# Where k and v of a batch are projected in a fused attention and feed-forward kernel

## The chip, the core and the metric

The kernel runs on one core of a Trainium2 chip. The core's engines work through their own instruction queues: PE (TensorE) multiplies matrices into PSUM, ACT (ScalarE) and DVE (VectorE) read PSUM and write SBUF, POOL (GpSimd) and SP issue transfers. PSUM has eight banks of 128 partitions by 512 fp32 values. The time of a run is the device time of one execution in microseconds, and the kernel's time is the median over runs.

## The reference

For 8 batches, 8 heads, 1024 positions and head dimension 64, with a sequence projection to 64 rows:

```python
k_proj = np.einsum('ks,bhsd->bhkd', E, k)
v_proj = np.einsum('ks,bhsd->bhkd', F, v)
scores = q @ k_proj^T / sqrt(64)
attn   = softmax(scores)
x      = attn @ v_proj            # heads side by side: 8192 x 512
h1, h2 = x @ w1, x @ w2           # 512 x 1024 each
out    = np.maximum(h1, h2) @ w_out   # 8192 x 512, float32
```

## The kernel before

**What is computed.** max(h1, h2) is h2 + relu(x (w1 - w2)), so the kernel forms wd = w1 - w2 and m = w2 w_out once; each block of positions then needs an *up* product, g = relu(x wd), and a *down* product, out = [g, x] [w_out; m]. Both are done as seven block products instead of eight (p1, p2, p6, p5, p7, p3, p4, in this order), from sums of blocks of x (`sums_x`) and of g (`sums_g`) that DVE forms beforehand, S(0) to S(3) of each. Operands are f16.

**Units and half units.** The 16 *units* are (batch, half of the positions), numbered n = 0 to 15. While unit n goes through its down products, unit n + 1 goes through its up products, and the attention of later positions is done in between. A unit in the middle is cut into two halves h = 0 and 1. The order of the work is written out by hand as a list of *slots*:
- `P`: a down product is cut in three *pieces* of four matmuls; 21 pieces make the unit, P0 to P20 below. The last piece of a product also issues what takes the result away. P0 to P2 are p1, P3 to P5 are p2, P6 to P8 are p6.
- `U`: the seven up products of a half, U0 to U6, four matmuls each.
- `G`: one attention *group* (`step_group`): 16 score matmuls for the next group, 8 for the softmax's denominators, 16 for the values of the present one. All use tiles of 64 rows by 32 columns of PE.

A half is: some pieces, G, some pieces, then U0, piece, U1, piece, ... U6. The pair in `for h, (x, y)` gives the pieces before and after G. Up to now it is (2, 2) in the first half and (2, 3) in the second, so a first half runs P0 P1 G P2 P3 U0 P4 U1 P5 U2 P6 U3 and so on.

Extra work is hung on slots with `at_slot(key, step)`; it is issued behind the slot's own work, in the order of the calls in the source. Every engine runs its instructions in the order of issue.

**PSUM.** Banks 0 and 1 belong to the down products, banks 2 and 3 to the up products, which share them with the group's scores. In odd units p1 of down is in bank 1 and p2 in bank 0; bank 0 was last read by ACT at the end of the unit before (L827). In the first half p1 and then p6, p7, p4 of up go to bank 2; p2 and then p5 and p3 to bank 3. U0's result is copied by ACT (`keep`, L610) before U2 adds onto the same bank; U1's result is added to it by DVE (L651) before U3 starts afresh in bank 3. The scores' two exps (L368) free banks 2 and 3 for U0 and U1. The other four banks are a ring of two double tiles, `att_banks`, for denominators (read by ACT's Ln, L389, issued within the group) and values (read by DVE at U2, L397).

ACT's queue in a first half is thus: two exps, Ln, the copy of P2's result, the copy of U0's result, the inversion of the denominators (L393), and further copies.

**k and v of a batch.** `step_kv` multiplies k and v by the projections in 16 matmuls of 512 columns, k into partitions 0 to 63 and v into 64 to 127 of one bank, in tiles of 128 rows by 64 columns. For batches b = 3 to 7 it is hung on U1 in the first half of unit n = 2b - 3 (n = 3, 5, 7, 9, 11) and uses a tile of the attention ring. ACT casts k out of the bank and writes it twice (L198), and SP issues a DMA transpose from there to `kpt` (L230), which the scores of G in the second half need. DVE casts v out of the bank (L206) and copies it to partitions 0 to 63 (L207); these two are put off by one slot (`return finish_v`). POOL waits for the transposes of q and for the second copy of k (`step_gate`) before it issues the loads of the next batch.

**DVE's sums.** S(0) of g and S(2) of x are hung on the last up slot of the unit before, S(1) of g on P0.

Of the kernel before, what the change touches and what calls it, by code (L numbers as in the profile page):

```python
# [16 lines left out]
def kernel(  # L17
# [12 lines left out]
    nc = tc.nc  # L30

    B, H, S, D = q.shape
    KP = E.shape[0]
# [25 lines left out]
    def mm_bank(dtype=FP32, n=None):  # L59
        if n is None:  # L60
            n = turn.pop(0)
            turn.append(n)
        return ps.tile([128, 512 if dtype == FP32 else 1024], dtype, tag=f"mm{n}", name="mm_ps")

    def att_banks(dtype=FP32):
        return ps.tile(
            [128, 2, 512 if dtype == FP32 else 1024], dtype, tag="att", bufs=2, name="att_ps"
        )
# [49 lines left out]
    for g in range(2):  # L118
        for w_sb, w in ((w2_sb, moe_w2), (w1_sb, moe_w1)):
            nc.gpsimd.dma_start(  # L120
                out=w_sb.rearrange("p (g z) f -> p g z f", z=2)[:, g, :, 0:256],
                in_=w.rearrange("(g p z) f -> p g z f", p=128, z=2)[:, g, :, 0:256],
            )
    for w_sb, w, f0, f1 in (
# [3 lines left out]
        for z in range(2):  # L128
            nc.gpsimd.dma_start(
                out=w_sb.rearrange("p (g z) f -> p g z f", z=2)[:, :, z, f0:f1],  # L130
                in_=w.rearrange("(g p z) f -> p g z f", p=128, z=2)[:, :, z, f0:f1],
# [22 lines left out]
    for i in range(2):  # L154
        eft_ps = mm_bank()
        for c in range(NC):
            nc.tensor.transpose(
                out=eft_ps[:, c * KP : (c + 1) * KP],
                in_=ef_sb[:, i].rearrange("k (p c) -> k c p", c=NC)[:, c, :],
# [3 lines left out]
        eng = nc.scalar.copy if i else nc.vector.tensor_copy  # L163
# [9 lines left out]


    def step_kv(t, h0=0, h1=H, which="kv", att=False, dma=False, copy=nc.vector.tensor_copy):
        kv_ps = att_banks()[:, 0, :] if att else mm_bank()
        n = (h1 - h0) * D
        both = which == "v"
        nh = 2 if both else h1 - h0
        for h in range(0, h1 - h0, nh):  # L180
            for c in range(NC):
                for w in which:
                    i = "kv".index(w)
                    for r in range(2) if both else (i,):
                        nc.tensor.matmul(  # L185
                            out=kv_ps[r * KP : (r + 1) * KP, h * D : (h + nh) * D],
                            lhsT=eft[i][:, c, :],
                            rhs=t[w][:, h0 + h : h0 + h + nh, c, :],
                            start=(c == 0), stop=(c == NC - 1),
                        )  # L190
        fl = lambda ap: ap[:, h0:h1].rearrange("p h z d -> p (h z d)")
        zd = lambda ap: ap.rearrange("p (h d z) -> p h z d", d=D // 2, z=2)
        if "k" in which:
            eng = nc.vector.tensor_copy if which == "k" else nc.scalar.copy
            kp = t["kp"][:, h0:h1]
            k_ps = kv_ps[0:KP, 0:n].rearrange("p (h d) -> p h d", d=D)
            if dma:
                eng(out=kp, in_=k_ps[:, :, None, :].broadcast_to([KP, h1 - h0, 2, D]))  # L198
                step_kpt_dma(t)
            else:  # L200
                eng(out=kp[:, :, 0, :], in_=k_ps)
        if both:
            copy(out=t["vp"][:, h0:h1], in_=zd(kv_ps[:, 0:n]))
        elif "v" in which:
            def finish_v():
                nc.vector.tensor_copy(out=t["vp"][KP:128, h0:h1], in_=zd(kv_ps[KP:128, 0:n]))  # L206
                nc.vector.tensor_copy(out=fl(t["vp"][0:KP]), in_=fl(t["vp"][KP:128]))  # L207

            if att:
                return finish_v  # L210
            finish_v()
# [17 lines left out]
    def step_kpt_dma(t):  # L229
        nc.sync.dma_start_transpose(  # L230
            out=t["kpt"], in_=t["kp"].rearrange("p h r d -> p (h r d)")
        )
# [235 lines left out]
    U = {(b, o): {"n": n, "b": b, "o": o, "t": tiles[b]} for n, (b, o) in enumerate(units)}  # L468
# [371 lines left out]
    t = tiles[0]  # L840
    new_attn(t)
    new_xt(t)
    step_kv(t, 0, 4, "k")
    warm(2)
    step_kpt(t, 0, 4)
# [5 lines left out]
    step_sc(t, 0, 1)  # L851
    warm(2)
    step_kv(t, 4, 8, "k")
    step_dn(t, 0, 0)
    warm(2)
# [7 lines left out]
    step_sc(t, 1, 0)  # L863
    step_sc(t, 1, 1)
    step_kv(t, 0, 4, "v")
    step_dn(t, 1, 0)
    step_inv(t, 1, 0)
# [48 lines left out]

    for n, key in enumerate(units):
        downs = down_steps(U[key], n == last)  # L920
        if n in (0, last):
            for p, pieces in enumerate(downs):
                slots += [(("P", n, p, i), x) for i, x in enumerate(pieces)]
            continue
        pieces = [(("P", n, p, i), x) for p, x in enumerate(downs) for i, x in enumerate(x)]
        ups = [*up_steps(U[units[n + 1]])]
        for h, (x, y) in enumerate(((6, 1), (2, 1)) if n == 1 else ((2, 2), (2, 3))):
            slots += pieces[:x]
            slots.append((("G", n, h), lambda: None))
            slots += pieces[x : x + y]  # L930
            del pieces[: x + y]
            for i in range(7):
                slots.append((("U", n, h, i), ups.pop(0)))
                if i < 6 - ((n, h) == (1, 0)):
                    slots.append(pieces.pop(0))
        assert not pieces and not ups
# [3 lines left out]
    def at_slot(key, s, *a):  # L940
        steps.setdefault(key, []).append(lambda: s(*a))
# [11 lines left out]
    t = tiles[1]  # L953
    at_slot((0, 22), new_attn, t)
    at_slot((0, 22), lambda: turn.__setitem__(slice(None), [2, 3]))
    for n, x in enumerate((
# [3 lines left out]
        key = ("P", n // 15, (n - 1) // 2 % 7, (n - 1) % 2) if n else (0, 22)  # L960
# [22 lines left out]
    t = tiles[2]  # L983
# [8 lines left out]
    for b in range(3, B):  # L992
        t = tiles[b]
        n = 2 * b - 3
        key = ("U", n - 1, 1, 5)
        at_slot(key, new_attn, t)
        at_slot(key, step_qt_dma, t, 0, H // 2)
        at_slot(key, step_qt_dma, t, H // 2, H)
        at_slot(("U", n, 0, 1), step_kv, t, 0, H, "kv", True, True)
        at_slot(("U", n, 0, 6), step_gate, t, "qt", H - 1)  # L1000
        at_slot(("U", n, 0, 6), step_gate, t, "kp", H - 1, 1)
        at_slot(("U", n, 0, 6), loads, b + 1, "k", "v", "q")
# [4 lines left out]
    for i, (new, old) in enumerate(zip([*groups[1:], none], groups)):  # L1007
        n, h = divmod(i + 2, 2)
# [8 lines left out]
    for n, (b, o) in enumerate(units):  # L1017
        u = U[b, o]

        if b == 0:  # L1020
            where = ()
        elif n == 2:
            where = (("P", 1, 1, 1), 0), (("P", 1, 1, 2), 1), (("P", 1, 2, 0), 2), (("U", 1, 0, 1), 3)
        else:
            where = tuple((("U", n - 2, 1, k), i) for k, i in ((6, 2), (3, 0), (4, 1), (5, 3)))
        for key, i in where:
            at_slot(key, sums_x, u, (i,))

        if n:
            end = ("U", n - 1, 1, 6) if n > 1 else ("P", 0, 6, 1)  # L1030
            m = 0 if n == last else 2
            for key, i in (end, 0), (("P", n, 0, 0), 1), (("P", n, 1, m), 2), (("P", n, 2, m), 3):
                at_slot(key, sums_g, u, (i,))

    pending = []
# [40 lines left out]
```

## Time and profile before

| | us |
|---|---|
| median of 6 runs (322.13 to 323.4) | 322.49 |
| the profiled execution | 322.27 |
| its span, first to last instruction | 320.5 |
| PE busy | 313.8 |
| DVE busy | 236.2 |
| ACT busy | 210.1 |
| POOL busy | 40.9 |
| start of the projection of batches 3 to 7 | 101.88, 137.50, 173.13, 208.75, 244.38 |

The starts of the projection are those in the chain that ended last. A timeline line holds start, duration, engine, source line, operation, output and inputs, the shapes, and how many instructions are merged in the line; in brackets stands how long the engine was idle before and which engine released it. The granted clock of PE was 0.999 of full speed.

### The profile page before, as it was taken

What the parts mean: (1) busy time and instruction counts of PE and PEld (TensorE: products, weight loads), DVE (VectorE), ACT (ScalarE), POOL (GpSimd) and SP (SyncE); (2) the same over time, 40 slices, a digit from 0 to 9 for tenths busy, and PEclk for the clock granted to TensorE, in tenths of its full rate; (3) what the DMA queues carried; (4) which work ended last, traced back from release to release, by engine and by line L of the source; (5) the groups of instructions that cost most, each with busy time, mean ns of one, the idle gap of its engine ahead of it and who ended that gap; (6) DMA issues with size and microseconds to landing.
All of it is one profiled execution on the core that took longest, in us unless ns stands there. A gap on an engine that the chain in (4) does not pass through costs nothing.

```text
span 320.5 us, 9138 instructions
## 1 busy us (share of the span) xinstructions
PE 313.8 (98%) x3910; PEld 250.9 (78%) x3910; DVE 236.2 (74%) x420; ACT 210.1 (66%) x374; POOL 40.9 (13%) x63
## 2 busy tenths in 40 slices
PE   8979999999999999999999999999999999999996
PEld 3554587878887888878887888878887888888885
DVE  1356789887967796876967796976967696969683
ACT  1376742767776777667776777667777777765541
POOL 8259102003000400021000400030000000000000
PEclk9999999999999999999999999999999999999999
DMA  7999999999959999799999899899969231303033
GB/s 142 206 200 189 200 205 203 207 192 155 206 107 162 176 208 245 198 194 160 232 209 215 159 204 245 207 164 177 230 133 215 51 100 36 100 33 101 33 101 130
DMA packets 76408, 53.14 MB, mean 166 GB/s; under 512 B 29520, under 2 KB 76240, under 8 KB 76368
## 3 DMA queue, kind: packets, MB, share of 16 engines
q0 software_dynamic: 30944, 28.31, 56.3%
q1 hardware_dynamic: 45056, 23.80, 31.0%
q8 instruction: 30, 0.49, 0.6%
q10 hardware_dynamic: 368, 0.46, 0.6%
q14 instruction: 10, 0.08, 0.1%
HBM read 57.15 MB, written 16.78 MB: 231 GB/s over the span
## 4 chain that ended last, share of the span: by engine, by line
PE 91%; DMA 6%; DVE 0%; POOL 0%; issue 0%; POOLq 0%; DVEq 0%
PE mm_ps L728 47%; PE mm_ps L636 27%; PE mm_ps L422 4%; PE att_ps L185 4%; DMA big<-in_moe_w_dram 4%; PE att_ps L285 3%; DMA q_sb<-in_q_dram 3%; PE mm_ps L273 2%; PE mm_ps L524 2%; PE mm_ps L244 1%; PE att_ps L447 0%; DVE o_sb L821 0%; PE mm_ps L447 0%; POOL k_sb L98 0%; PE att_ps L273 0%
## 5 line engine op out<-in xcount | busy, mean ns | idle before, releaser
L610 ACT COPY p_sb<-mm_ps 128x512 f32<-128x512 f32 x179 | 101.4, 593 | 44.4 <-PE mm_ps L636 27.7
L728 PEld LDWEIGHTS <-big 128*128 128x128 f16 x768 | 73.5, 98 | 12.2 <-issue 3.6
L728 PE MATMUL mm_ps<-T_sb,big 128*128 128x256 f16 x576 | 77.7, 273 | 0.0
L651 DVE TENSOR_TENSOR gt_sb<-mm_ps,p_sb 128x512 f16<-128x512 f32 x56 | 38.5, 688 | 43.4 <-PE mm_ps L636 43.3
L636 PE MATMUL mm_ps<-big,big 128*128 128x256 f16 x336 | 50.4, 272 | 0.0
L636 PEld LDWEIGHTS <-big 128*128 128x128 f16 x448 | 43.8, 98 | 5.1
L728 PE MATMUL mm_ps<-wo_sb,gt_sb 128*128 128x256 f16 x256 | 42.8, 273 | 0.0
L728 PEld LDWEIGHTS <-gt_sb 128*128 128x128 f16 x376 | 35.2, 98 | 9.0 <-issue 5.0
L636 PEld LDWEIGHTS <-wd_sb 128*128 128x128 f16 x336 | 32.9, 98 | 3.8
L636 PE MATMUL mm_ps<-xt_sb,wd_sb 128*128 128x256 f16 x224 | 33.6, 273 | 0.0
L368 ACT ACTIVATE ex_sb<-mm_ps 128x512 f16<-128x512 f32 x50 | 27.2, 596 | 8.8 <-PE att_ps L285 7.5
L397 DVE TENSOR_TENSOR xt_sb<-att_ps,ld_sb 128x1024 f16<-128x1024 f32 x26 | 31.7, 1219 | 0.1
L758 DVE TENSOR_TENSOR o_sb<-mm_ps,p_sb 128x512 f32<-128x512 f32 x32 | 21.9, 685 | 9.3 <-PE mm_ps L728 7.3
L236 POOL COPY junk<-qt_sb 1x1 f16<-1x1 f16 x6 | 2.4, 402 | 172.9 <-DMA qt_sb<-q_sb 172.9
L728 PE MATMUL mm_ps<-m_sb,xt_sb 128*128 128x256 f16 x128 | 24.4, 273 | 0.0
L697 ACT ACTIVATE gt_sb<-mm_ps 128x512 f16<-128x512 f32 x28 | 16.8, 600 | 9.0 <-PE mm_ps L636 9.0
L654 DVE TENSOR_SCALAR gt_sb<-gt_sb 128x512 f16<-128x512 f16 (+1 forms) x60 | 21.1, 352 | 2.1
L596 DVE TENSOR_TENSOR big<-gt_sb 128x1024 f16<-128x1024 f16 x32 | 21.9, 684 | 0.1
L728 PE MATMUL mm_ps<-wo_sb,big 128*128 128x256 f16 x128 | 21.5, 272 | 0.0
L728 PE MATMUL mm_ps<-T_sb,gt_sb 128*128 128x256 f16 x120 | 20.3, 273 | 0.0
L728 PEld LDWEIGHTS <-xt_sb 128*128 128x128 f16 x188 | 18.4, 98 | 2.2
L651 DVE TENSOR_TENSOR gt_sb<-p_sb 128x512 f16<-128x512 f32 x28 | 19.1, 682 | 0.7 <-ACT p_sb L610 0.6
(104 smaller groups left out, 432.4 us busy)
## 6 DMA issues: line engine op xcount, KB each, us to landing
out_dram<-o_sb SPq DMA_DIRECT2D x62, 256.0 KB, 2.7
k_sb<-in_k_dram POOLq DMA_DIRECT2D x7, 1024.0 KB, 9.7
v_sb<-in_v_dram POOLq DMA_DIRECT2D x7, 1024.0 KB, 16.1
q_sb<-in_q_dram POOLq DMA_DIRECT2D x5, 1024.0 KB, 23.1
q_sb<-in_q_dram POOLq DMA_DIRECT2D x6, 512.0 KB, 15.5
big<-in_moe_w_dram POOLq DMA_DIRECT2D x12, 128.0 KB, 6.3
k_sb<-in_k_dram POOLq DMA_DIRECT2D x2, 512.0 KB, 8.3
v_sb<-in_v_dram POOLq DMA_DIRECT2D x4, 256.0 KB, 14.1
```

Source lines behind the costliest of these rows:

```text
L185: nc.tensor.matmul(out=kv_ps[r * KP : (r + 1) * KP, h * D : (h + nh) * D], lhsT=eft[i][:, c, :], rhs=t[w][:, h0 + h : h0 + h + nh, c, :], ...
L368: nc.scalar.activation(out=t["ex", g, j][:, e, :], in_=banks[e], func=ACTF.Exp, scale=scale)
L397: nc.vector.tensor_tensor(out=x_out(t, g, j).rearrange("q z o n -> q o z n"), in0=at_ps.rearrange("q o (z n) -> q o z n", z=2), in1=ld[:, ...
L422: nc.tensor.matmul(out=h_ps, lhsT=wd_sb[:, r, fb * 128 : (fb + 1) * 128], rhs=t["xt"][:, r, :, j * W : (j + 1) * W], start=(r == 0), stop= ...
L596: nc.vector.tensor_tensor(out=S(i), in0=S(0) if x is None else x, in1=y(), op=op)
L610: copy(out=x, in_=bank)
L636: nc.tensor.matmul(out=bank[:, m * W : (m + 1) * W], lhsT=w_[:, n_, (2 * d + m) * 128 : (2 * d + m + 1) * 128], rhs=a[:, n_, :], start=(n ...
L651: nc.vector.tensor_tensor(out=c_blk(j, c), in0=two(x), in1=two(y), op=ALU.add)
L654: nc.vector.tensor_scalar_max(ap, ap, 0.0)
L697: nc.scalar.activation(out=out, in_=in_, func=ACTF.Relu)
L728: nc.tensor.matmul(out=bank[i][:, 0:CH] if two_banks else bank[:, i * CH : (i + 1) * CH], lhsT=a(c)[:, i * 128 : (i + 1) * 128], rhs=w_(c) ...
L758: nc.vector.tensor_tensor(out=o_sb, in0=two(x), in1=two(y), op=ALU.add)
```

## The change

For batches 3 to 7 the projection moves from U1 to G in the first half of the same unit, ahead of the group's own matmuls. It uses bank 0 instead of a tile of the attention ring. k is cast by DVE instead of ACT, once instead of twice, and DVE makes the second copy in SBUF; the DMA transpose is issued behind that. The copies are no longer put off by a slot. The order on DVE is: k cast, v cast to partitions 64 to 127, second copy of k, v copy to partitions 0 to 63. In these five units S(1) of g moves from P0, and S(2) of x from the last up slot of the unit before, to the slot of G, behind the copies. The pieces around the two groups become (2, 1) and (3, 3), so that the first half runs P0 P1 projection G P2 U0 P3 U1 P4 U2 P5 U3 P6 and so on.

```diff
     def step_kv(t, h0=0, h1=H, which="kv", att=False, dma=False, copy=nc.vector.tensor_copy):
-        kv_ps = att_banks()[:, 0, :] if att else mm_bank()
+        kv_ps = att_banks()[:, 0, :] if att else mm_bank(n=0 if dma else None)
...
         if "k" in which:
-            eng = nc.vector.tensor_copy if which == "k" else nc.scalar.copy
+            eng = nc.vector.tensor_copy if which == "k" or dma else nc.scalar.copy
             kp = t["kp"][:, h0:h1]
-            k_ps = kv_ps[0:KP, 0:n].rearrange("p (h d) -> p h d", d=D)
-            if dma:
-                eng(out=kp, in_=k_ps[:, :, None, :].broadcast_to([KP, h1 - h0, 2, D]))
-                step_kpt_dma(t)
-            else:
-                eng(out=kp[:, :, 0, :], in_=k_ps)
+            eng(out=kp[:, :, 0, :], in_=kv_ps[0:KP, 0:n].rearrange("p (h d) -> p h d", d=D))
...
                 nc.vector.tensor_copy(out=t["vp"][KP:128, h0:h1], in_=zd(kv_ps[KP:128, 0:n]))
+                if dma:
+                    nc.vector.tensor_copy(out=kp[:, :, 1, :], in_=kp[:, :, 0, :])
+                    step_kpt_dma(t)
                 nc.vector.tensor_copy(out=fl(t["vp"][0:KP]), in_=fl(t["vp"][KP:128]))
...
+    kv_units = range(3, 2 * B - 4, 2)
...
-        for h, (x, y) in enumerate(((6, 1), (2, 1)) if n == 1 else ((2, 2), (2, 3))):
+        cut = ((6, 1), (2, 1)) if n == 1 else ((2, 1), (3, 3)) if n in kv_units else ((2, 2), (2, 3))
+        for h, (x, y) in enumerate(cut):
...
-        at_slot(("U", n, 0, 1), step_kv, t, 0, H, "kv", True, True)
+        at_slot(("G", n, 0), step_kv, t, 0, H, "kv", False, True)
...
-            where = tuple((("U", n - 2, 1, k), i) for k, i in ((6, 2), (3, 0), (4, 1), (5, 3)))
+            two = ("G", n - 1, 0) if n - 1 in kv_units else ("U", n - 2, 1, 6)
+            where = ((two, 2), *((("U", n - 2, 1, k), i) for k, i in ((3, 0), (4, 1), (5, 3))))
...
-            for key, i in (end, 0), (("P", n, 0, 0), 1), (("P", n, 1, m), 2), (("P", n, 2, m), 3):
+            one = ("G", n, 0) if n in kv_units else ("P", n, 0, 0)
+            for key, i in (end, 0), (one, 1), (("P", n, 1, m), 2), (("P", n, 2, m), 3):
                 at_slot(key, sums_g, u, (i,))
```

## The prediction

> **What bounds the kernel now.** I read the page's shares and its chain first, then the timeline of each engine through one of the five half units that the change touches (batch 4, unit 5; the other four repeat it at a period of 35.6 us).
>
> ```profile
> PE 313.8 (98%) x3910; PEld 250.9 (78%) x3910; DVE 236.2 (74%) x420; ACT 210.1 (66%) x374; POOL 40.9 (13%) x63
> ...
> PE 91%; DMA 6%; DVE 0%; POOL 0%; issue 0%; POOLq 0%; DVEq 0%
> ```
>
> PE carries the chain after the start-up, and in the steady part nothing keeps it waiting. So each 0.1 us that PE loses or saves in a touched half unit is 0.5 us of the kernel; time on ACT, DVE or POOL counts only where PE has to wait for it.
>
> PE around the group and the projection:
>
> ```profile
> 134.16 0.38 PE L728 MATMUL mm_ps<-wo_sb,gt_sb 128*128 128x256 f16 x2
> 134.47 0.41 PE L273 MATMUL mm_ps<-qt_sb,kpt_sb 64*32 64x256 f16 x16
> ...
> 135.14 0.39 PE L728 MATMUL mm_ps<-wo_sb,gt_sb 128*128 128x256 f16 x2
> ...
> 136.90 0.60 PE L636 MATMUL mm_ps<-xt_sb,wd_sb 128*128 128x256 f16 x4
> 137.43 0.40 PE L185 MATMUL att_ps<-k_sb,eft 128*64 128x512 f16 x1
> ...
> 139.28 0.39 PE L728 MATMUL mm_ps<-wo_sb,gt_sb 128*128 128x256 f16 x2
> ...
> 139.73 0.60 PE L636 MATMUL mm_ps<-big,big 128*128 128x256 f16 x4
> 140.16 0.60 PE L728 MATMUL mm_ps<-T_sb,big 128*128 128x256 f16 x4
> 140.60 0.60 PE L636 MATMUL mm_ps<-big,big 128*128 128x256 f16 x4
> ```
>
> A set of four 128*128 matmuls takes 0.44 us (140.16 to 140.60), which I call a step. U1 starts at 136.90 and should end at 137.34; the projection starts at 137.43. From there to U2 at 139.73 are 2.30 us, of which a step is 0.44 and eight pairs of 512 columns at 0.214 are 1.71. So this excursion to narrow tiles costs 0.09 + 0.15 = 0.24 us beyond its matmuls. The group pays its own entry: two matmuls from 134.16 end at 134.38 and the scores start at 134.47.
>
> ACT and DVE in the same stretch:
>
> ```profile
> 134.94 1.09 ACT L368 ACTIVATE ex_sb<-mm_ps 128x512 f16<-128x512 f32 x2 [0.58 <-PE att_ps L285]
> 135.91 0.60 ACT L389 ACTIVATE ld_sb<-att_ps 128x512 f32<-128x512 f32 x1
> 136.39 1.09 ACT L610 COPY p_sb<-mm_ps 128x512 f32<-128x512 f32 x2
> ...
> 139.42 1.01 ACT L198 CAST kp_sb<-att_ps 64x1024 f16<-64x1024 f32 x1 [1.41 <-PE att_ps L185]
> ```
>
> ```profile
> 133.47 0.68 DVE L651 TENSOR_TENSOR gt_sb<-mm_ps,p_sb 128x512 f16<-128x512 f32 x1
> 134.07 0.68 DVE L651 TENSOR_TENSOR gt_sb<-p_sb 128x512 f16<-128x512 f32 x1
> ...
> 135.46 0.68 DVE L596 TENSOR_TENSOR big<-gt_sb 128x1024 f16<-128x1024 f16 x1
> 136.07 0.42 DVE L596 TENSOR_TENSOR big<-xt_sb 128x512 f16<-128x512 f16 x1
> ...
> 139.93 0.69 DVE L758 TENSOR_TENSOR o_sb<-mm_ps,p_sb 128x512 f32<-128x512 f32 x1 [1.30 <-PE mm_ps L728]
> 140.65 0.69 DVE L206 CAST vp_sb<-att_ps 64x512 f16<-64x512 f32 x1
> 141.38 0.29 DVE L207 COPY vp_sb<-vp_sb 64x512 f16<-64x512 f16 x1
> 141.69 0.69 DVE L596 TENSOR_TENSOR big<-gt_sb 128x1024 f16<-128x1024 f16 x1
> ```
>
> On ACT the two exps, Ln, and the copies of P2 and U0 run without a gap: the U0 copy ends at 137.48, 3.01 us after the scores began. U2 writes the same bank and today comes at 139.73, with the projection before it, so the copy is hidden. On DVE a full-height operation after another starts 0.60 us later (133.47 to 134.07), but around the half-height copies nothing overlaps: 0.72, 0.73 and 0.31 us for operations of 0.69, 0.69 and 0.29.
>
> **The change, part by part.** Times count from the switch to narrow tiles, 134.47 today and unchanged: P1 ends there as before. ACT's L827 copy out of bank 0 has started by 133.27 and takes 0.59, so the bank is free at 133.9.
>
> *PE.* Projection 1.85 (137.43 to 139.28, exit included), then the group. A direct passage from the projection's tiles to the group's is seen once in start-up: sixteen 128-column matmuls from 19.42, eight pairs at 0.05, should end at 19.85, and the sums start at 19.99, 0.14 later; the exit today is 0.10. I take 0.10, already in the 1.85; the bounds are 0 and a whole excursion, 0.24. Scores at 1.85, P2 at 2.52 (0.67, as 134.47 to 135.14), U0 2.97, P3 3.41, U1 3.84, P4 4.28, U2 4.71, P5 5.15, U3 5.58, and after the moved step 6.02. Today the same work ends at 140.60, which is 6.13. Without any wait the change saves 0.11, five times 0.55 us.
>
> [...]
>
> *ACT.* It loses the 1.01 us cast, which bounds nothing. But the cut (2, 1) leaves one step between group and U0 where there were two, and the projection no longer stands between U0 and U2. The five operations take 3.01 from the scores, so the U0 copy ends at 4.86; with 0.05 for the signal (start-up: ACT's vp copy ends 23.04, the matmul starts 23.09) U2 starts at 4.91, not 4.71. That wait of 0.20 puts U3 at 5.78.
>
> *DVE.* It gains a k cast and a duplicate. No row shows either: the cast is bounded by its double, L206 at 0.69, and ACT's 1.01; the duplicate by L207 at 0.29 (same size, f16) and 0.69. I take 0.69 and 0.29, the nearest forms. Starts at the spacing of the half-height rows: k cast 1.99 (ACT started its own 1.99 after the first matmul; DVE is idle from 1.68, after the sum of 135.46), high v cast 2.71, duplicate 3.43, low v copy 3.75, S(1) of g 4.06, S(2) of x 4.67, U1's add 5.11, done at 5.80. Bank 0 is free at 3.40, so P3 waits to 3.45 instead of 3.41, inside the wait at U2. The add frees bank 3, which U3 overwrites: with the signal 5.85 against 5.78. U3 waits another 0.07. Today that add starts at 137.61 and U3 comes at 140.60. After it DVE catches up: relu, the 1.22 us xt product and the o_sb add end near 7.9, and P9 needs that bank at 8.9.
>
> [...]
>
> *Other queues.* The sums come after the copies but before need: S(1) at 4.8 for P6 (6.3), S(2) at 5.1 for U4 (6.7). SP now meets the kpt transpose behind two qt transposes (133.88, 4.74 us) and one store (138.72, 1.20): issue at 139.9 instead of 140.45, landing 2.7 later (at most 4.2), before the scores that need it at 144.96; SP's later stores move with it and nothing waits for them. POOL's gate reads the duplicate, long written; its loads wait for qt. k and v are read 2.96 us earlier: the v load issued at 143.83 lands by 163.3 at the longest row (19.5), the next projection is at 170.1; for batch 3 it is 95.6 against 98.8. The attention ring has one tile fewer; its users were not waiting. Each costs nothing under this cover; a v load 3.2 us later would stop PE for the excess.
>
> *Sum.* U3 at 5.85 plus the moved step is 6.29, against 6.13: 0.16 per half unit, 0.8 us for five. The profiled execution took 322.27 us (span 320.5), 0.22 below the median; it would become 323.07, and the median 322.49 becomes 323.3.
>
> **The rivals.**
> - *Faster: the banks come in time.* The U0 copy would have to be done before 4.71 and the add before 5.58. For: DVE's chain at full overlap ends at 5.3. Against: ACT's five operations have no gap to give. Then the shared excursion decides: 0.11 to 0.24 each, 0.55 to 1.2 us, 321.3 to 321.9. It decides from a U0 copy that ends 0.15 earlier.
> - *ACT's wait alone.* If DVE frees bank 3 before 5.78, the loss is 0.09, 0.45 us: 322.9, not to be told from no change (0.2% or 0.65 us is about what a measurement can tell). For: 0.07 is a small margin. Against: the half-height spacings.
> - *DVE much later.* A duplicate at 0.69 puts the add 0.40 later and the loss at 0.56: 2.8 us, 325.3; half of that gives 323.3 + 1.0 = 324.3. Against: L207 at 0.29.
>
> **How the numbers follow.** My case (DVE's add decides, 322.9 to 323.7) 0.47, of which 0.10 falls within 0.2%; ACT alone 0.20, nearly all within (0.18); DVE much later 0.13, slower; banks in time 0.20, of which 0.18 faster. So faster 0.18, within 0.30, slower 0.52. The range of 8 in 10 reaches from 321.7, inside the faster case, to 324.8, inside the late duplicate.
>
> **What would show it.** Projection followed by the scores 1.85 later; the exps 0.47 after them; U2 about 0.2 late behind ACT's copy; U3 at 5.8 to 5.9 behind the add; k cast 0.69 and duplicate 0.29; P3 on time within 0.05. The prediction is wrong if PE steps follow each other at 0.44 through U2 and U3, or if the passage to the scores costs other than 0.1.

## The result and the profile after

The changed kernel takes 323.12 us (median of 30 runs) against 322.33 us for the kernel before (64 runs beside it): a ratio of 1.0033, with a 95% interval of 1.002 to 1.0047. The medians differ by 0.8 us, and the interval reaches from 0.6 to 1.5 us; 0.8 us had been predicted, and from the median of the first six runs, 322.49, a time of 323.3 us.

The page of the changed kernel looks like that of the one before: PE is busy for 98% of the span and carries the chain.

```profile
PE 315.6 (98%) x3910; PEld 251.4 (78%) x3910; DVE 239.5 (74%) x430; ACT 205.2 (64%) x369; POOL 40.4 (13%) x63
...
PE 94%; DMA 3%; ACT 1%; DVE 1%; issue 0%; DVEq 0%; POOLq 0%
```

What ACT and DVE have of the chain lies in the start-up (13.9 to 24.6 us) and in the last microseconds (from 319.1 us), so neither line shows a wait in the steady part. The list of PE's waits does not help either; of the kernel after, its longest two lines are both from the start-up:

```profile
PE mm_ps L143 <- DVE ones L136: 1.5, 1, 1.5
PE mm_ps L185 <- DMA k_sb<-in_k_dram: 1.1, 1, 1.1
```

The second is a late first load of this one execution, whose span (322.8) is 2.3 us above that of before (320.5) though the medians differ by 0.8. Of that, 1.41 us lie ahead of P0 of unit 3, which starts at 99.29 instead of 97.88; behind the late load the granted clock from 10 to 20 us was 0.83, where the kernel before had 1.00. The executions differ in the start-up, so traces are compared here by one stretch: from the start of P0 of unit 3 to the start of P0 of unit 13, which holds the five half units of the change. That is 276.01 - 97.88 = 178.13 us for the kernel before and 278.31 - 99.29 = 179.02 for the changed one: 0.89 us more.

The loss has to be read from the starts of PE's lines. This is PE in the half unit of batch 4, in the changed kernel, whose line numbers after the diff are lower by two (L726 is a step of down, L634 of up). The projection's first matmul starts at 136.03.

```profile
135.71 0.38 PE L726 MATMUL mm_ps<-wo_sb,gt_sb 128*128 128x256 f16 x2
136.03 0.40 PE L185 MATMUL mm_ps<-k_sb,eft 128*64 128x512 f16 x1
...
137.87 0.41 PE L271 MATMUL mm_ps<-qt_sb,kpt_sb 64*32 64x256 f16 x16
...
138.99 0.60 PE L634 MATMUL mm_ps<-xt_sb,wd_sb 128*128 128x256 f16 x4
139.47 0.60 PE L726 MATMUL mm_ps<-wo_sb,gt_sb 128*128 128x256 f16 x4
139.91 0.60 PE L634 MATMUL mm_ps<-xt_sb,wd_sb 128*128 128x256 f16 x4
...
140.56 0.38 PE L726 MATMUL mm_ps<-wo_sb,gt_sb 128*128 128x256 f16 x2
140.94 0.60 PE L634 MATMUL mm_ps<-big,big 128*128 128x256 f16 x4
...
141.59 0.38 PE L726 MATMUL mm_ps<-m_sb,xt_sb 128*128 128x256 f16 x2
141.87 0.60 PE L634 MATMUL mm_ps<-big,big 128*128 128x256 f16 x4
```

Where nothing waits, steps of four matmuls follow each other at 0.44 (140.16 to 140.60 in the kernel before, 142.74 to 143.18 in this one), sets of two at 0.22 (140.34 to 140.56). From U0 (138.99) to P3 (139.47) are 0.48, from the last two matmuls of P4 (140.56) to U2 (140.94) 0.38, and from the last two of P5 (141.59) to U3 (141.87) 0.28. So P3 waits 0.04, U2 another 0.16 and U3 another 0.06. PE's line stays busy through all three, because the ends that the profile gives for the matmuls reach the next starts or overlap them (140.56 and 0.38 make 140.94).

What each waited for stands in ACT's and DVE's lines of the same stretch:

```profile
138.34 1.08 ACT L366 ACTIVATE ex_sb<-mm_ps 128x512 f16<-128x512 f32 x2 [2.43 <-PE att_ps L283]
139.31 0.60 ACT L387 ACTIVATE ld_sb<-att_ps 128x512 f32<-128x512 f32 x1
139.79 1.10 ACT L608 COPY p_sb<-mm_ps 128x512 f32<-128x512 f32 x2
```

```profile
138.01 0.68 DVE L196 CAST kp_sb<-mm_ps 64x512 f16<-64x512 f32 x1 [0.31 <-PE mm_ps L185]
138.73 0.69 DVE L201 CAST vp_sb<-mm_ps 64x512 f16<-64x512 f32 x1
139.45 0.28 DVE L203 COPY kp_sb<-kp_sb 64x512 f16<-64x512 f16 x1
139.77 0.29 DVE L205 COPY vp_sb<-vp_sb 64x512 f16<-64x512 f16 x1
140.07 0.69 DVE L594 TENSOR_TENSOR big<-big,gt_sb 128x1024 f16<-128x1024 f16 x1
140.68 0.42 DVE L594 TENSOR_TENSOR big<-xt_sb 128x512 f16<-128x512 f16 x1
141.13 0.69 DVE L649 TENSOR_TENSOR gt_sb<-mm_ps,p_sb 128x512 f16<-128x512 f32 x1
```

The high v cast ends at 139.42 and P3 starts at 139.47. The two L608 copies, of P2 and U0, end at 140.89 and U2 starts at 140.94. U1's add ends at 141.82 and U3 starts at 141.87. Each time PE starts 0.05 us after the reader of the bank has finished.

### The profile page after: what moved, and what is told of

It reads as the page before. It is cut to its first block, busy times and chain, and to the rows that moved or that the text cites. A ratio compares the mean times of both kernels' runs of the same rounds, so it can differ in the third digit from the quotient of the medians.

```text
span 322.8 us, 9143 instructions
## 1 busy us (share of the span) xinstructions
PE 315.6 (98%) x3910; PEld 251.4 (78%) x3910; DVE 239.5 (74%) x430; ACT 205.2 (64%) x369; POOL 40.4 (13%) x63
## 4 chain that ended last, share of the span: by engine, by line
PE 94%; DMA 3%; ACT 1%; DVE 1%; issue 0%; DVEq 0%; POOLq 0%
PE mm_ps L726 46%; PE mm_ps L634 27%; PE mm_ps L420 4%; PE mm_ps L185 4%; PE att_ps L283 3%; DMA k_sb<-in_k_dram 3%; PE mm_ps L271 2%; PE mm_ps L522 2%; PE att_ps L185 1%; PE mm_ps L143 1%; PE mm_ps L242 1%; ACT ex_sb L311 1%; PE att_ps L271 0%; DVE qt_sb L247 0%; ACT ld_sb L323 0%; PE att_ps L445 0%
## 5 line engine op out<-in xcount | busy, mean ns | idle before, releaser
L608 ACT COPY p_sb<-mm_ps 128x512 f32<-128x512 f32 x179 | 101.8, 593 | 51.3 <-PE mm_ps L634 28.8
L726 PEld LDWEIGHTS <-big 128*128 128x128 f16 x768 | 73.3, 98 | 12.4 <-issue 3.6
L726 PE MATMUL mm_ps<-T_sb,big 128*128 128x256 f16 x576 | 77.0, 273 | 0.0
L634 PE MATMUL mm_ps<-big,big 128*128 128x256 f16 x336 | 50.4, 273 | 0.0
L634 PEld LDWEIGHTS <-big 128*128 128x128 f16 x448 | 43.7, 98 | 6.3 <-issue 0.3
L726 PE MATMUL mm_ps<-wo_sb,gt_sb 128*128 128x256 f16 x256 | 42.8, 273 | 0.0
L726 PEld LDWEIGHTS <-gt_sb 128*128 128x128 f16 x376 | 35.5, 98 | 7.5 <-issue 2.9
L634 PEld LDWEIGHTS <-wd_sb 128*128 128x128 f16 x336 | 32.8, 98 | 3.9
L634 PE MATMUL mm_ps<-xt_sb,wd_sb 128*128 128x256 f16 x224 | 33.6, 273 | 0.0
L726 PE MATMUL mm_ps<-m_sb,xt_sb 128*128 128x256 f16 x128 | 24.4, 273 | 0.0
L234 POOL COPY junk<-qt_sb 1x1 f16<-1x1 f16 x6 | 1.4, 228 | 174.3 <-DMA qt_sb<-q_sb 174.3
L652 DVE TENSOR_SCALAR gt_sb<-gt_sb 128x512 f16<-128x512 f16 (+1 forms) x60 | 20.9, 348 | 2.1
L726 PE MATMUL mm_ps<-wo_sb,big 128*128 128x256 f16 x128 | 21.5, 273 | 0.0
L726 PE MATMUL mm_ps<-T_sb,gt_sb 128*128 128x256 f16 x120 | 20.3, 273 | 0.0
L726 PEld LDWEIGHTS <-xt_sb 128*128 128x128 f16 x188 | 18.4, 98 | 2.2
```

Source lines behind the costliest of these rows:

```text
L608: copy(out=x, in_=bank)
L634: nc.tensor.matmul(out=bank[:, m * W : (m + 1) * W], lhsT=w_[:, n_, (2 * d + m) * 128 : (2 * d + m + 1) * 128], rhs=a[:, n_, :], start=(n ...
L652: nc.vector.tensor_scalar_max(ap, ap, 0.0)
L726: nc.tensor.matmul(out=bank[i][:, 0:CH] if two_banks else bank[:, i * CH : (i + 1) * CH], lhsT=a(c)[:, i * 128 : (i + 1) * 128], rhs=w_(c) ...
```

## The experiments

Times named with a sign are the difference of the stretch from P0 of unit 3 to P0 of unit 13 against the kernel before, in one execution each, read from starts given to 0.01 us; ratios are of timed runs against the kernel before, with 95% intervals. In the expectations, times like 4.91 or 5.78 count from the projection's first matmul.

**One wait taken away: S(2) of x behind U1's add** (on the changed kernel)

```diff
-            two = ("G", n - 1, 0) if n - 1 in kv_units else ("U", n - 2, 1, 6)
+            two = ("P", n - 1, 1, 1) if n - 1 in kv_units else ("U", n - 2, 1, 6)
```

> In the five half units S(2) of x goes behind U1's add and relu on DVE; all else is the changed kernel. Theory A (two bank waits, the later one decides; no wait of DVE's or ACT's load as such): the add starts 0.34 earlier, bank 3 is free at 5.5 after the switch to narrow tiles, U2 still waits for ACT to 4.91, so U3 comes at 5.78 instead of 5.85: the loss goes from 0.16 to 0.09 per half unit, the kernel from +0.8 to about +0.45 us against the kernel before. Theory B (DVE's added work costs by its length, wherever it stands): nothing changes, +0.8 us.

Measured, from a first matmul at 134.93:

```profile
139.84 0.60 PE L634 MATMUL mm_ps<-big,big 128*128 128x256 f16 x4
...
140.71 0.60 PE L634 MATMUL mm_ps<-big,big 128*128 128x256 f16 x4
```

U2 comes at 4.91 and U3 at 5.78. The stretch is +0.43 us, the ratio 1.0016 (0.9993 to 1.004). DVE does the same work as in the changed kernel, so half of the loss went with the order of two operations, not with their length. The timed interval alone would not have told this from no change; the starts do.

**The other wait taken away: Ln behind the copy of U0** (on the changed kernel)

```diff
                 t2, g2, j2, lambda: (new() if first else acts)(), (g, j) == (0, 0) and t is tiles[2]
+                or (g, j) == (1, 1) and any(t is tiles[b] for b in range(2, B - 1))
...
-        if (n, h) == (1, 1):
+        if (n, h) == (1, 1) or (h == 0 and n in kv_units):
             at_slot(("U", n, h, 1), step_later)
```

> In the five half units ACT's Ln comes after the copy of U0, the inversion after U1; all else is the changed kernel. Theory A: the U0 copy ends 0.48 earlier, U2 comes at 4.75 (P3 still waits 0.04 for bank 0) and not at 4.91, but U3 still waits for DVE's add to 5.85: the wait moves from U2 to U3 and the time stays at +0.8 us. Theory C (ACT's wait at U2 is the loss, U3 only inherits it): U3 at 5.62, the time falls to about -0.35 us against the kernel before.

Measured, from a first matmul at 134.26:

```profile
139.02 0.60 PE L635 MATMUL mm_ps<-big,big 128*128 128x256 f16 x4
140.11 0.60 PE L635 MATMUL mm_ps<-big,big 128*128 128x256 f16 x4
```

U2 comes at 4.76, so ACT's wait is gone, but U3 still comes at 5.85, behind DVE's add (139.37, 0.69 long). The stretch is +0.91 us, the ratio 1.0031 (1.0014 to 1.0048): nothing is won. The two waits do not add up; the later one decides.

**Both taken away** (the two edits above together)

> Both of the moves of the other two kernels together. Theory A: U2 at 4.75, bank 3 free at 5.5, U3 at 5.62, only P3's 0.04 left: -0.07 per half unit, -0.35 us against the kernel before. If the two waits were separate costs that add up, taking each away alone would already have given its own share; if neither is the cause, +0.8 us stays.

Measured, from a first matmul at 134.13:

```profile
138.89 0.60 PE L635 MATMUL mm_ps<-big,big 128*128 128x256 f16 x4
...
139.76 0.60 PE L635 MATMUL mm_ps<-big,big 128*128 128x256 f16 x4
```

U2 comes at 4.76 and U3 at 5.63. The stretch is -0.14 us, the ratio 0.9996 (0.9977 to 1.0015). The loss is gone, but the gain is 0.2 less than expected. P3, whose wait for the v cast was left, shows where most of it went: it waits 0.04 in batches 3 and 4 but 0.10, 0.10 and 0.07 in batches 5, 6 and 7 (more on that at the end).

**The cut (1, 2)** (on the changed kernel), run in two series

```diff
-        cut = ((6, 1), (2, 1)) if n == 1 else ((2, 1), (3, 3)) if n in kv_units else ((2, 2), (2, 3))
+        cut = ((6, 1), (2, 1)) if n == 1 else ((1, 2), (3, 3)) if n in kv_units else ((2, 2), (2, 3))
```

> The first half unit is cut (1, 2) instead of (2, 1): P0, projection, group, P1, P2, U0, P3 and so on; nothing else. Theory A: two steps between group and U0 again, so U2 comes 0.44 later after the scores than in the changed kernel and the U0 copy (3.01 after the scores) is done; P3 comes 0.44 later than bank 0 needs; the add is done before U3. No wait is left, and the excursion saved shows alone: -0.11 per half unit, -0.55 us against the kernel before. If the passage from the projection to the scores costs a whole excursion, 0 us; if it costs nothing, -1.2 us. Where the projection starts one step earlier, bank 0 is just free of ACT's copy; if that is late, PE waits before the projection and the gain shrinks.

> The kernel with the cut (1, 2) once more, to narrow its interval against the kernel before. Theory A: -0.55 us, a ratio of 0.9983; the first series had a median 0.33 us lower and a ratio of 1.0 with an interval of 0.4% about it.

Measured in the first series, first matmul at 134.19:

```profile
136.04 0.41 PE L271 MATMUL mm_ps<-qt_sb,kpt_sb 64*32 64x256 f16 x16
...
137.60 0.60 PE L634 MATMUL mm_ps<-xt_sb,wd_sb 128*128 128x256 f16 x4
138.47 0.60 PE L634 MATMUL mm_ps<-xt_sb,wd_sb 128*128 128x256 f16 x4
139.34 0.60 PE L634 MATMUL mm_ps<-big,big 128*128 128x256 f16 x4
140.22 0.60 PE L634 MATMUL mm_ps<-big,big 128*128 128x256 f16 x4
```

U0, U1, U2 and U3 follow each other at 0.87, two steps each, with no wait. The stretch is -0.53 us, and -0.45 in the second series. In the first the starts of the projection lie 35.52 apart, four times the same, against 35.62 or 35.63 in the kernel before. In the second they lie 35.52, 35.61, 35.51 and 35.53 apart: in batch 4 a wait is back, outside the half unit, at the group of the second half.

```profile
144.21 0.40 PE L283 MATMUL att_ps<-ex_sb,vp_sb 64*32 64x256 f16 x16
144.50 0.14 PEld L271 LDWEIGHTS <-kpt_sb 64*32 64x32 f16 x16 [0.17 <-DMA kpt_sb<-kp_sb]
```

The weights of the scores are what the DMA transpose of k writes. It was issued at 139.52 and took 4.9 us to land, and the scores start 0.29 after the first of the values' matmuls instead of 0.21 in the first series, where the transpose took 4.7. In batch 4 the transfer landed 0.4 us ahead of the scores in the kernel before (issued at 140.45, 4.2 to land, scores at 144.96), 0.7 ahead in the changed kernel, 0.1 in the first series and not at all in the second. Why it takes longer to land was not tested.

The ratio is 1.0 (0.9978 to 1.0022) in the first series and 0.9981 (0.9969 to 0.9993) in the second, 321.59 against 322.1 us. So by the second series this version is 0.1 to 0.3% faster than the kernel before, and the first does not tell it from no change; beside the changed kernel it was not timed. It has the shared excursion of the change without the waits at P3, U2 and U3.

**The projection apart from the group, no wait** (both edits that take the waits away, and)

```diff
-        at_slot(("G", n, 0), step_kv, t, 0, H, "kv", False, True)
+        at_slot(("P", n, 0, 0), step_kv, t, 0, H, "kv", False, True)
```

> The kernel with S(2) of x and Ln later (both waits gone), and in addition the projection one step ahead of the group's slot: P0, projection, P1, group, P2. All that differs from the kernel with the cut (1, 2) in PE's total is then that projection and group are two excursions. Theory A: no wait, no shared excursion: 0.0 us against the kernel before, 0.11 per half unit or 0.55 us slower than the cut (1, 2). If sharing had saved a whole excursion, 0.24 per half unit would separate the two, 1.2 us; if the waits had other causes, this one would show them again.

Measured: the stretch is 178.14 us against 178.13 in the kernel before; the ratio is 0.9997 (0.9984 to 1.0009). Against the cut (1, 2) of the first series, 177.60, sharing one excursion between projection and group is worth 0.54 us, 0.11 in each of five half units.

**The cut alone** (on the kernel before: (2, 1), (3, 3) in units 3, 5, 7, 9, 11 and nothing else)

> The kernel before with nothing but the cut (2, 1), (3, 3) in the five units; projection on U1, k copied by ACT. Theory A: U0 comes one step earlier, but the projection still stands between U0 and U2, 1.95 us of PE work, so the U0 copy (3.01 after the scores) is long done: 0.0 us against the kernel before. If the cut itself costs (theory D, U0 too close to the group's exps), +0.2 per half unit, up to +1 us.

Measured: 0.00 us, ratio 0.9999 (0.9983 to 1.0014). U0's step closer to the group costs nothing as long as the projection stands behind it.

**DVE's copies alone** (on the kernel before)

```diff
-            eng = nc.vector.tensor_copy if which == "k" else nc.scalar.copy
+            eng = nc.vector.tensor_copy if which == "k" or dma else nc.scalar.copy
...
-                eng(out=kp, in_=k_ps[:, :, None, :].broadcast_to([KP, h1 - h0, 2, D]))
+                eng(out=kp[:, :, 0, :], in_=k_ps)
+                nc.vector.tensor_copy(out=kp[:, :, 1, :], in_=kp[:, :, 0, :])
```

> The kernel before with k cast once by DVE and duplicated by DVE (0.69 + 0.29 us of DVE work per batch in place of ACT's 1.01); projection on U1 in the attention ring, cut unchanged. Theory A: no PE step waits on it there: 0.0 us. Theory B (DVE's added work costs by its length): up to 0.98 per batch, +4.9 us, and by the share that the changed kernel would need, +0.8 us.

Theory A missed. The stretch is +1.77 us, the ratio 1.0053 (1.0035 to 1.0072). U2 and U3 are on time; the loss sits at the group of the second half. PE and DVE there, of this kernel (L274 scores, L729 down, L652 U5's two adds):

```profile
145.19 0.73 PE L274 MATMUL mm_ps<-qt_sb,kpt_sb 64*32 64x256 f16 x16
145.85 1.37 PE L729 MATMUL mm_ps<-T_sb,big 128*128 128x256 f16 x11
```

```profile
144.18 0.68 DVE L597 TENSOR_TENSOR big<-gt_sb,big 128x1024 f16<-128x1024 f16 x1
144.78 0.68 DVE L652 TENSOR_TENSOR gt_sb<-mm_ps,p_sb 128x512 f16<-128x512 f32 x1
145.38 0.68 DVE L652 TENSOR_TENSOR gt_sb<-p_sb 128x512 f16<-128x512 f32 x1
```

From the scores to the next step are 0.66 us, where the kernel before takes 0.34. The same places in the kernel before:

```profile
144.96 0.40 PE L273 MATMUL mm_ps<-qt_sb,kpt_sb 64*32 64x256 f16 x16
145.30 1.48 PE L728 MATMUL mm_ps<-T_sb,big 128*128 128x256 f16 x12
```

```profile
144.13 0.68 DVE L651 TENSOR_TENSOR gt_sb<-mm_ps,p_sb 128x512 f16<-128x512 f32 x1
```

The scores write bank 3, which U5's first add reads until 145.46; the first scores start at 145.19, the next ones only at 145.51, 0.05 behind the add:

```profile
145.51 0.29 PE L274 MATMUL mm_ps<-qt_sb,kpt_sb 64*32 64x256 f16 x5
```

In the kernel before that add ended at 144.81, only 0.15 ahead of the scores. That reading was tested by itself.

**The same, with S(3) of g behind U5's adds** (on the kernel just shown)

```diff
-            for key, i in (end, 0), (("P", n, 0, 0), 1), (("P", n, 1, m), 2), (("P", n, 2, m), 3):
+            for key, i in (end, 0), (("P", n, 0, 0), 1), (("P", n, 1, m), 2), (("P", n, 3, 1) if n in range(3, 2 * B - 4, 2) else ("P", n, 2, m), 3):
```

> The kernel before with k cast and duplicated by DVE, as in the run that came out 0.34 us per half unit slower, and with S(3) of g moved behind U5's two adds and relu. Theory E (in that run DVE's added 0.98 us makes U5's first add late, 144.78 to 145.46, and the second group's scores, which start at 145.19, wait for it to free bank 3): the add comes 0.60 earlier, ends near 144.9 and the scores no longer wait: 0.0 us against the kernel before. Theory B (added DVE work costs by its length): the same 1.7 us as in that run, since DVE does the same work.

Measured, in the same half unit, which starts 1.15 us later in this execution:

```profile
146.34 0.40 PE L274 MATMUL mm_ps<-qt_sb,kpt_sb 64*32 64x256 f16 x16
146.67 1.48 PE L729 MATMUL mm_ps<-T_sb,big 128*128 128x256 f16 x12
```

```profile
145.31 0.68 DVE L652 TENSOR_TENSOR gt_sb<-mm_ps,p_sb 128x512 f16<-128x512 f32 x1
145.91 0.68 DVE L652 TENSOR_TENSOR gt_sb<-p_sb 128x512 f16<-128x512 f32 x1
```

The add ends at 145.99, the scores start at 146.34 and the next step 0.33 later. The stretch differs by 0.00 us, the ratio is 0.9996 (0.9986 to 1.0005). DVE does the same 0.98 us of added work per batch as before the edit: it costs nothing where no bank waits for it, and 0.33 to 0.40 us a batch where one does.

## Why the prediction was right

**The sum.** 0.16 us per half unit, 0.8 in all, was predicted; the medians differ by 0.79 and the stretches by 0.89. From P0 of a touched unit to P0 of the next unit the loss is 0.15 in batches 3 and 4 and 0.22, 0.20 and 0.18 in batches 5 to 7. That the medians meet 0.8 so closely is in part luck: the interval reaches from 0.6 to 1.5 us. The steps of the sum are what the traces show right.

**The passage to the scores**, taken as 0.10 inside 1.85: the scores start at 1.84. The saving without any wait, taken as 0.11, is measured by the cut (1, 2) against the kernel with the two apart: 0.11. So the passage is neither free, which would have saved the whole excursion of 0.24, nor an excursion of its own, which would have saved nothing: one excursion in place of two is worth 0.11 us per half unit (177.60 against 178.14 us by the stretches, over five). What PE does in the passage no row shows.

**ACT's wait at U2**, predicted at 4.91, is at 4.91, and the exps start 0.47 after the scores as predicted. The reason given, one step between group and U0 in place of two with the projection gone from between U0 and U2, has both halves shown: the cut alone costs nothing, the cut (1, 2) removes the wait.

**DVE's add at U3**, predicted to end at 5.80 and to let U3 start at 5.85: it ends 5.79 after the first matmul (141.82) and U3 starts at 5.84. The two unknown prices were near: k cast 0.68 for 0.69, duplicate 0.28 for 0.29. The spacings of the half-height copies, 0.72, 0.72, 0.32 and 0.30, are those of the rows of before, not the 0.60 of full-height operations; overlap is back only between the two sums (140.07 to 140.68, 0.61 for 0.69). The 0.44 from S(2) of x to the add (4.67 to 5.11) is not settled by the rows of before, which have both 0.45 (132.68 to 133.13) and 0.33 (136.07 to 136.40) behind operations of 0.42; it was 0.45 (140.68 to 141.13). With 0.1 us less at each of the five spacings other than that between the sums, the add would have ended about 0.5 us earlier; this estimate from the rows is also the 5.3 of the faster rival. Why the spacings differ no run shows.

**P3**, predicted 0.04 late behind the v cast: 0.04 in batches 3 and 4, and 0.07 to 0.11 in the other three.

**The rivals.** "ACT's wait alone" was 0.07 away, and moving one sum turned the kernel into it (+0.43 for the 0.45 predicted for that rival). "The banks come in time" is what the cut (1, 2) made of it, at the lower end of that rival's 0.55 to 1.2 us. That rival left out the signal that the sum counts: with 0.05 for it the U0 copy has to end by 4.66 and not by 4.71, and so 0.20 earlier and not 0.15. A late duplicate did not happen.

**Where it was off.** The stretch lost 0.09 us more than the sum. In batches 5, 6 and 7 U3 comes 4.07, 4.06 and 4.03 after the scores, in batches 3 and 4 4.00 as predicted. The term is the start of the k cast, taken as 1.99 for all five: it starts 0.14 after the scores in batches 3 and 4 and 0.21, 0.20 and 0.17 in the others. The transpose of k was given at most 4.2 us to land; in batch 4 it took 4.4 in the changed kernel, which left 0.7 us before the scores, and 4.9 in the second trace of the cut (1, 2), which left none. And one bank was not looked at, bank 3 at the group of the second half. At the old place the same copies make PE wait 0.33 to 0.40 us a batch there; at the new place DVE has caught up by then, as the prediction said (U5's first add, at 144.40 and 0.68 long, ends 1.6 us ahead of the scores at 146.67), so its sum did not need that bank. The expectation of the copies alone did, and missed.

## What to carry to other kernels

Where PE has no gap at all, read its starts against the ideal spacing, not its busy share or its list of waits: the bank readers that kept PE waiting for 0.04 to 0.16 us here showed in neither. For every step that comes earlier, list the bank that it overwrites and walk the queue of the engine that reads it, operation by operation. Here two banks were late one behind the other, only the later counted, and taking away the other wait alone won nothing. Look at transfers in the same way: the transpose of k, 0.7 us ahead of its reader in the changed kernel, was just too late in one trace of the faster one. A cut that restores the distance between a product and its copy can be worth more than the move itself: here the cut (1, 2) was 1.42 us better than the changed kernel by the stretches (0.89 and 0.53), where the shared excursion by itself is worth 0.54.

## What the runs showed of the hardware

One thing was unexpected. The k cast on DVE has a separate semaphore instruction ahead of it in three batches of the five, in the changed kernel as on ACT in the kernel before (L198 there: x3, 172.3 to 243.6):

```profile
L196 DVEq EVENT_SEMAPHORE  x3: 21/1090/1110, 173.8 to 244.4; - x3
```

Their first and last starts, 173.8 and 244.4, put them in batches 5 to 7, the same in which the cast starts 0.03 to 0.07 us later after the scores than in batches 3 and 4. In the run with DVE's copies alone these three lose 0.40, 0.38 and 0.36 us at the second group, and batches 3 and 4 lose 0.33. That the extra instruction is the cause was not tested; nor was what it waits for.
